# A three-part fused block on one core: operands of the channel stage recomputed or made in place instead of kept in DRAM

## The chip, the cores and the metric

The kernel runs on one core of one Trainium2 chip. The metric is device time in microseconds (us) of one execution, as the median of several runs. Three runs of the kernel before gave 974.24, 976.15 and 978.49 us. The profiled execution, from which every duration below is taken, took 970.43 us.

## The reference

The computation is three blocks, one after the other, on a batch of 4 with 448 tokens (S) and 768 channels, all in float32:

```python
# 1. attention, 12 heads of 64, scores capped with tanh
s = cap * tanh(scale * (q @ k.T) / cap);  x = softmax(s) @ v
# 2. gated block
h = relu(x @ w_in)                        # 768 -> 1024
x = (h * sigmoid(conv3(h, conv_w))) @ w_out   # -> 768
# 3. token and channel mixing
u = x + (relu(x.T @ w_tok1) @ w_tok2).T   # token stage, 448 -> 256 -> 448
y = u + relu(u @ w_ch1) @ w_ch2           # channel stage, 768 -> 1536 -> 768
```

The weights of blocks 2 and 3 come as float64 and have to be narrowed to float32 on the chip. The change is in the last line, the channel stage.

## The kernel before, in words

**Precision.** A float32 product is made of three fast matmuls: each operand is split into a rounded high part and the remainder (`split3`: high x high, high x low, low x high). A split costs one ScalarE copy (the high part) and one VectorE subtraction (the low part), and the split operand is twice as large as what it was made from.

**The channel stage.** The 1536 hidden channels are cut in three thirds t of four blocks; the batch in two pairs p of two elements. Six stages s run in the order (t, p) = (0,0), (0,1), (1,1), (1,0), (2,0), (2,1), so that between neighbours either the pair or the third changes. I call them s=0 to s=5. A stage has two halves:

- `up` runs twice, once for each unit u of two hidden blocks (u = 2t, 2t+1). A Strassen-like scheme makes the 2x2 block product with seven products of nine matmuls each (`product`, L888) instead of eight. It needs seven combinations of input blocks, the operands of the input ("B11", "T1" and so on, `UB`, made by `u_make`: L794 on ScalarE, L795 and L804 on VectorE, from loads of `u_d` into tiles `c`, L801), and seven combinations of weight blocks, the first weights' operands (`W1`, placed in tiles named wi_h and wi_l). VectorE adds the products up (L893) and ScalarE and VectorE make the split relu (`relu`, L879 and L880).
- `down` runs twice, for the two batch elements, over six blocks m of output channels: twelve matmuls (L926) from the split hidden values and the second weights (`w2`), then VectorE adds (L927) the partial result v, which was loaded from DRAM (L921), and stores it again (L928; `v_d`, in the last third `out`). v lies in one of four tiles that rotate (`temp`).

The tiles of one unit's seven W1 operands are used again by the unit of the next third; those of `w2` and of the input's operands likewise.

**What is kept in DRAM.** Three things are made once, stored split, and loaded when needed:

- `us_d`: the 21 operand tiles (seven by three k) of pair 0's input. They are stored as they are made (L797) and loaded for s=3, during the `down` of s=2 (`u_load`, L831), when the pair changes back from 1 to 0. For pair 1 they are made from `u_d` with `u_all`, each time.
- `w1_d`: the split W1 operands of units 2 to 5 (28 tiles). Units 0 and 1 go straight into place. The others are written to a staging tile (`staging`, two of them), stored (L639), and loaded in `down` of the last stage of a third (`w1_load`, L868).
- `w2_d`: the split second weights (24 halves), through staging (L673), loaded at the start of each third (`w2_load`, L874).

**Making weights.** A job narrows one 128x384 block (`block`: load L619, one ScalarE instruction L620, three VectorE instructions L621 to L623, into a tile ba, bb or bx, each one buffer deep), and then makes from it one or more splits (`parts`, L609 and L610) and sums. A unit takes four jobs, a block of second weights two. The jobs of the first third run during the token stage before. The 32 of the others are put into the program in the stages, at every step of `up` and `down`, in numbers that the table `JOBS` sets:

```python
JOBS = 5, 11, 9, 7, 0, 0
...
due += JOBS[s] / 26
while due >= 1:
    due -= 1
    wc_step(st_pools)
```

What is still left is flushed before the loads that need it.

**Order.** The program is written in the order of these loops, and the framework's scheduler lays out each engine's instructions from it, in one fixed order per engine. All DMAs of this part are issued by SP (SyncE) in one queue, in order: a DMA whose source is not ready holds up those behind it.

Of the kernel before, what the change touches and what calls it, by code (L numbers as in the profile page):

```python
# [20 lines left out]
KD = DM // 128  # L21
# [9 lines left out]
QK = S + KW  # L31
JOBS = 5, 11, 9, 7, 0, 0
YTB = 9
# [270 lines left out]
def fused_kernel(ctx, tc, ins, out, attention):  # L304
# [5 lines left out]
    v_d = [PRE.tile([B, KD, 128, S], F32, name=f"v_d{i}", tag=f"v_d{i}") for i in range(2)]  # L310
    w1_d = PRE.tile([MC // 2, 7, 128, 768], F32, name="w1_d")
    w2_d = PRE.tile([MC, 2, 128, 768], F32, name="w2_d")
    us_d = PRE.tile([7, 3, 128, 2 * S], F32, name="us_d")
    wide = {n: ins[n].bitcast(U32) for n in ("w_in", "conv_w", "w_out", "w_tok1", "w_tok2", "w_ch1", "w_ch2")}
# [311 lines left out]
    def unit_jobs(u):  # L626
# [4 lines left out]
        def put(name, t):  # L631
            o = ORDER.index(name)
            if u < 2:
                W1[u, o] = place_of(u, o)
                parts(t, W1[u, o])
            else:
                w = staging()
                parts(t, w)
                nc.sync.dma_start(w1_d[u, o], w.bitcast(F32))  # L639

# [27 lines left out]
    def w2_jobs(c):  # L668
        def job(pools, i):
            t = block(pools, wide["w_ch2"][c, :, 768 * i : 768 * i + 768], "bx")  # L670
            w = staging()
            parts(t, w)
            nc.sync.dma_start(w2_d[c, i], w.bitcast(F32))  # L673

        return [lambda pools, i=i: job(pools, i) for i in range(2)]

    def third_jobs(t):
        return [j for u in (2 * t, 2 * t + 1) for j in unit_jobs(u)] + [j for c in range(4 * t, 4 * t + 4) for j in w2_jobs(c)]

# [70 lines left out]
    while True:  # L750
# [6 lines left out]
        if n >= WCS and not begun:  # L757
            begun = True
            todo.extend(third_jobs(0))
        if n > TKS:  # L760
# [24 lines left out]

    def u_make(p, k, want, keep):


        def put(name, t):
            if name not in want:  # L790
                return
            o = BORDER.index(name)
            w = u_tile(o, k)
            nc.scalar.copy(w[:, 0], t)  # L794
            nc.vector.tensor_tensor(w[:, 1], t, w[:, 0].bitcast(F32), op=ALU.subtract)  # L795
            if keep:
                nc.sync.dma_start(us_d[o, k], flat(w).bitcast(F32))  # L797

# [24 lines left out]

    def u_all(p, want, keep):
        for k in range(3):
            yield from u_make(p, k, want, keep)

    def u_load():
        for o in range(7):
            for k in range(3):  # L830
                nc.sync.dma_start(flat(u_tile(o, k)).bitcast(F32), us_d[o, k])  # L831
                yield

    toks.append(tokens(B - 1))
    first = u_all(0, BORDER[0:3], True)
    while toks:
# [27 lines left out]

    def w1_load(u):
        for o in range(7):
            W1[u, o] = place_of(u, o)
            nc.sync.dma_start(W1[u, o].bitcast(F32), w1_d[u, o])  # L868

    def w2_load(c):  # L870
        pool = Gm if c % 4 < 2 else Gb
        w2[c] = pool.tile([128, 2, 2, 384], F32R, name=f"w2_{c % 4}", tag=f"w2_{c % 4}")
        for i in range(2):
            nc.sync.dma_start(w2[c][:, i].rearrange("p t n -> p (t n)").bitcast(F32), w2_d[c, i])  # L874

# [41 lines left out]
    def down(t, p, j):  # L917
        b = 2 * p + j
        for m in range(KD):
# [3 lines left out]
            for r in range(4):  # L923
                w, h = w2[4 * t + r][:, m // 3, :, m % 3 * 128 : m % 3 * 128 + 128], hs[r, j]
                for n, (l, x) in enumerate(split3(w[:, 0], w[:, 1], h[:, 0], h[:, 1])):
                    nc.tensor.matmul(ps[:, 0:S], l, x, start=r == 0 and n == 0, stop=r == 3 and n == 2)  # L926
# [3 lines left out]

    for _ in u_all(0, BORDER[3:7], True):
        pass
    for c in range(4):
        w2_load(c)
    todo.extend(third_jobs(1) + third_jobs(2))
    order = [(0, 0), (0, 1), (1, 1), (1, 0), (2, 0), (2, 1)]
    due = 0.0
    for s, (t, p) in enumerate(order):
        nt, np_ = order[s + 1] if s < 5 else (t, p)

        def tick():
            nonlocal due
            due += JOBS[s] / 26
            while due >= 1:
# [3 lines left out]
        for i in range(2):  # L948
            for n, _ in enumerate(up(2 * t + i)):
                if i == 0 and n == 0 and s and t != order[s - 1][0]:  # L950
                    wc_step(st_pools, len(todo) - 16 * (2 - t))
                    for c in range(4 * t, 4 * t + 4):
                        w2_load(c)
                tick()
        coming = iter(())
        if np_ != p:
            coming = u_load() if s == 2 else u_all(np_, BORDER, False)
        for j in range(2):
            for m, _ in enumerate(down(t, p, j)):
                for _ in range(2):  # L960
                    next(coming, None)
                if nt != t and m == 3:
                    wc_step(st_pools, len(todo) - 16 * (2 - nt) - 8)
                    w1_load(2 * nt + j)
                tick()
        for _ in coming:
            pass


# [73 lines left out]
```

## Time and profile before

| what | value |
|---|---|
| median of three runs | 976.15 us (974.24 to 978.49) |
| the profiled execution | 970.43 us |
| its span | 968.3 us |
| TensorE matmul busy (PE) | 887.6 us, 92% |
| VectorE busy (DVE) | 684.3 us, 71% |
| ScalarE busy (ACT) | 492.8 us, 51% |
| TensorE clock granted, mean | 0.966 of full speed |
| moved by DMA | 216.91 MB, mean 224 GB/s |

The span is the profiled execution from its first instruction to its last; 2.1 us lie around it. The chain that ended last is put to PE for 42% of the span, to DMA for 22%, to DVE for 20%, to ACT for 8%. In the slices of the span PE is at 9 tenths or more nearly everywhere, with two dips in the last 400 us (6 to 7 tenths), and the DMA engines are at 8 to 9 tenths through that part, where they stood at 1 to 7 before. Averages over the span say little here, because the last 400 us, the channel stage, are a stage of their own.

### The profile page before, as it was taken

To read this page: it belongs to the slowest core of one execution; us is meant where nothing else is said; L and a number is where in the kernel's file an instruction comes from. 1 tells how busy PE (TensorE), PEld (TensorE's weight loads), DVE (VectorE), ACT (ScalarE), POOL (GpSimd) and SP (SyncE) were. 2 spreads that over 40 slices of the span, in tenths; PEclk is the share of its full clock that TensorE was granted. 3 is DMA by queue.
4 is the path that set the end of the run, shared out by engine and by line. 5 is a ranking of instruction groups with operands and counts; after the bars stand their busy time and mean duration, and the time that the engine had idled before them with its cause. 6 is when DMAs were issued, how large, how long until landed. Compare 5 with 4: busy or idle time off the path is not lost.

```text
span 968.3 us, 12321 instructions
## 1 busy us (share of the span) xinstructions
PE 887.6 (92%) x4105; PEld 762.9 (79%) x4105; DVE 684.3 (71%) x1244; ACT 492.8 (51%) x817; POOL 4.2 (0%) x19
## 2 busy tenths in 40 slices
PE   7989999989999999989999797799996678999997
PEld 4655888868998898879888686689895567898996
DVE  6769989789866887468976655998648326749542
ACT  6979888777876787437543322444213102214210
POOL 0000000000000000000000000000000000000000
PEclk9999999989999999999999988899999889999999
DMA  7665555755155422573588889889999889897324
GB/s 270 202 212 186 174 187 176 246 197 168 57 181 208 156 91 66 176 231 114 170 282 298 301 295 353 269 275 338 302 321 301 312 297 328 295 338 233 120 86 146
DMA packets 95833, 216.91 MB, mean 224 GB/s; under 512 B 13618, under 2 KB 54546, under 8 KB 93458
## 3 DMA queue, kind: packets, MB, share of 16 engines
q1 hardware_dynamic: 95762, 216.05, 66.5%
q8 instruction: 34, 0.56, 0.2%
q14 instruction: 37, 0.30, 0.1%
HBM read 149.19 MB, written 63.90 MB: 220 GB/s over the span
## 4 chain that ended last, share of the span: by engine, by line
PE 42%; DMA 22%; DVE 20%; ACT 8%; issue 5%; SPq 3%; DVEq 0%; ACTq 0%
PE mm L926 9%; PE mm L488 7%; PE mm L462 6%; PE o L888 5%; DMA c<-u_d 3%; PE ps_s L146 2%; DMA w_raw<-in_w_out 2%; PE ps_s L147 2%; DMA u_d<-yt 2%; DMA rr<-v_d 2%; PE ps_e L722 2%; PE ps_e L736 1%; DMA raw<-in_qk 1%; DMA sel<-in_w_ch 1%; DMA w_raw<-in_w_ch 1%
## 5 line engine op out<-in xcount | busy, mean ns | idle before, releaser
L926 PE MATMUL mm<-hs,w 128*128 128x448 f32 x864 | 192.3, 380 | 29.3 <-DVE sums L927 14.2
L926 PEld LDWEIGHTS mm<-hs,w 128*128 128x128 f32 x864 | 167.0, 195 | 51.1 <-DVE sums L927 16.4
L488 PE MATMUL mm<-gh,wo 128*128 128x448 f32 x384 | 128.8, 376 | 7.2 <-ACT wo L358 3.5
L462 PE MATMUL mm<-xx,wi_h 128*128 128x448 f32 x384 | 115.2, 370 | 0.5 <-DVE xx L449 0.5
L488 PEld LDWEIGHTS mm<-gh,wo 128*128 128x128 f32 x384 | 73.2, 192 | 17.0 <-ACT wo L358 5.3
L146 PE MATMUL ps_s<-ab 128*128 128x448 f32 x192 | 82.5, 431 | 3.3 <-DVE ab L115 3.0
L462 PEld LDWEIGHTS mm<-xx,wi_h 128*128 128x128 f32 x384 | 71.8, 188 | 9.2 <-issue 2.0
L168 ACT ACTIVATE a<-ps_s,icap 128x896 f32<-128x896 f32 x76 | 66.9, 884 | 23.1 <-PE ps_s L147 18.6
L488 PE MATMUL mm<-gl,wo 128*128 128x448 f32 x192 | 71.7, 373 | 0.3 <-DVE gl L477 0.3
L147 PE MATMUL ps_s<-low,ab 128*128 128x448 f32 x192 | 71.4, 373 | 0.0
L169 ACT ACTIVATE a<-a,cap 128x896 f32<-128x896 f32 x76 | 70.2, 925 | 1.2
L462 PE MATMUL mm<-xx,wi_l 128*128 128x448 f32 x192 | 70.3, 366 | 0.0
L176 DVE TENSOR_TENSOR al<-a,ah 128x896 fp32r<-128x896 f32 (+1 forms) x56 | 54.4, 973 | 3.2
L888 PE MATMUL o<-u,wi_h 128*128 128x448 f32 x216 | 51.0, 368 | 1.5 <-ACT u L794 1.3
L175 DVE CAST ah<-a 128x896 fp32r<-128x896 f32 (+1 forms) x56 | 31.6, 566 | 28.8 <-ACT a L169 13.5
L888 PE MATMUL o<-u,wi_l 128*128 128x448 f32 x216 | 49.1, 364 | 2.5 <-DMA u<-us_d 0.9
L888 PE MATMUL o<-xx,wi_l 128*128 128x448 f32 x162 | 39.7, 375 | 8.5 <-ACT xx L794 5.3
L146 PEld LDWEIGHTS ps_s<-ab 128*128 128x128 f32 x192 | 36.7, 192 | 13.2 <-issue 5.5
L888 PEld LDWEIGHTS o<-u,wi_h 128*128 128x128 f32 x216 | 40.8, 190 | 6.2 <-ACT u L794 2.7
L888 PEld LDWEIGHTS o<-u,wi_l 128*128 128x128 f32 x216 | 40.2, 188 | 6.4 <-DMA u<-us_d 1.3
L111 ACT CAST ab<-raw 128x960 fp32r<-128x960 f32 x38 | 37.2, 989 | 15.8 <-DMA raw<-in_qk 9.7
L620 ACT ACTIVATE w_pt<-w_raw 128x384 f32<-128x384 f32 x32 | 17.6, 551 | 51.7 <-DMA w_raw<-in_w_ch 46.9
(161 smaller groups left out, 1677.2 us busy)
## 6 DMA issues: line engine op xcount, KB each, us to landing
raw<-in_qk SPq DMA_DIRECT2D x20, 960.0 KB
wo<-wo_d SPq DMA_DIRECT2D x18, 1024.0 KB
w_raw<-in_w_ch SPq DMA_DIRECT2D x32, 384.0 KB
c<-u_d SPq DMA_DIRECT2D x48, 224.0 KB
w_d<-wi_l SPq DMA_DIRECT2D x26, 384.0 KB
w_d<-wi_h SPq DMA_DIRECT2D x26, 384.0 KB
w<-w_d SPq DMA_DIRECT2D x24, 384.0 KB
w_raw<-in_w_in SPq DMA_DIRECT2D x16, 384.0 KB
```

The costliest lines, as they stand in the source:

```text
L111: nc.scalar.copy(h, r)
L146: nc.tensor.matmul(ps[:, bank, 0:S], a[:, keys], a[:, 0:S], start=start, stop=False)
L147: nc.tensor.matmul(ps[:, bank, 0:S], a[:, keys], low, start=False, stop=stop)
L168: nc.scalar.activation(a[:, 0:n], ps[:, 0:n, 0:S], AF.Tanh, scale=self.c["icap"])
L169: nc.scalar.activation(a[:, 0:n], a[:, 0:n], AF.Exp, scale=self.c["cap"])
L175: nc.vector.tensor_copy(ah[:, 0:n], a[:, 0:n])
L176: nc.vector.tensor_tensor(al[:, 0:n], a[:, 0:n], ah[:, 0:n].bitcast(F32), op=ALU.subtract)
L462: nc.tensor.matmul(ps[:, 0:S], w, v, start=k == 0 and n == 0, stop=k == KD - 1 and n == 2)
L488: nc.tensor.matmul(ps[:, 0:S], w, v, start=k == 0 and n == 0, stop=k == MF - 1 and n == 2)
L722: nc.tensor.matmul(ps[:, 0:384], l, r, start=c == 0 and n == 0, stop=c == NS - 1 and n == 1)
L888: nc.tensor.matmul(ps, l, r, start=k == 0 and n == 0, stop=k == 2 and n == 2)
L926: nc.tensor.matmul(ps[:, 0:S], l, x, start=r == 0 and n == 0, stop=r == 3 and n == 2)
```

## The change

- `u_load` and `us_d` go. At each change of the pair (s=0, s=2, s=4) the input's 21 operands are made anew with `u_all`, from twelve loads of `u_d`; it advances by one step per m of `down` where it advanced by two.
- `w1_d` and `w1_load` go. Each unit's jobs write their splits straight into the tiles of `W1`. The jobs of the next third's first unit enter the program when the first `up` of a third's last stage is through (its tiles are free then), those of the second unit after the second `up`.
- `w2_d` holds float32, not splits: a job stores its 128x384 block from the tile bx itself (half of the bytes). `w2_load` loads a whole block of 128x768 into a staging tile and splits it there, one ScalarE and one VectorE instruction of 128x768; for the later thirds it does that at steps 2 to 5 of the first `up`.
- `JOBS` goes. In s=0 and s=2 eight jobs of second weights are spread over 26 steps, in s=1 and s=3 the eight of the next third's units over 19.

```diff
-            if u < 2:
-                W1[u, o] = place_of(u, o)
-                parts(t, W1[u, o])
-            else:
-                w = staging()
-                parts(t, w)
-                nc.sync.dma_start(w1_d[u, o], w.bitcast(F32))
+            W1[u, o] = place_of(u, o)
+            parts(t, W1[u, o])
...
             t = block(pools, wide["w_ch2"][c, :, 768 * i : 768 * i + 768], "bx")
-            w = staging()
-            parts(t, w)
-            nc.sync.dma_start(w2_d[c, i], w.bitcast(F32))
+            nc.sync.dma_start(w2_d[c, :, 384 * i : 384 * i + 384], t)
...
-        return [j for u in (2 * t, 2 * t + 1) for j in unit_jobs(u)] + [j for c in range(4 * t, 4 * t + 4) for j in w2_jobs(c)]
+        return [j for c in range(4 * t, 4 * t + 4) for j in w2_jobs(c)]
...
-            if keep:
-                nc.sync.dma_start(us_d[o, k], flat(w).bitcast(F32))
...
-    def w1_load(u):
-        for o in range(7):
-            W1[u, o] = place_of(u, o)
-            nc.sync.dma_start(W1[u, o].bitcast(F32), w1_d[u, o])
...
         pool = Gm if c % 4 < 2 else Gb
-        w2[c] = pool.tile([128, 2, 2, 384], F32R, name=f"w2_{c % 4}", tag=f"w2_{c % 4}")
-        for i in range(2):
-            nc.sync.dma_start(w2[c][:, i].rearrange("p t n -> p (t n)").bitcast(F32), w2_d[c, i])
+        t = staging().bitcast(F32)
+        nc.sync.dma_start(t, w2_d[c])
+        w2[c] = w = pool.tile([128, 2, KD * 128], F32R, name=f"w2_{c % 4}", tag=f"w2_{c % 4}")
+        nc.scalar.copy(w[:, 0], t)
+        nc.vector.tensor_tensor(w[:, 1], t, w[:, 0].bitcast(F32), op=ALU.subtract)
...
+        due, rate = 0.0, 0.0
+        if s % 2 == 0 and t < 2:
+            todo.extend(third_jobs(t + 1))
+            rate = 8.5 / 26
...
             for n, _ in enumerate(up(2 * t + i)):
-                if i == 0 and n == 0 and s and t != order[s - 1][0]:
-                    wc_step(st_pools, len(todo) - 16 * (2 - t))
-                    for c in range(4 * t, 4 * t + 4):
-                        w2_load(c)
+                if s % 2 == 0 and s and i == 0 and 2 <= n < 6:
+                    w2_load(4 * t + n - 2)
                 tick()
-        coming = iter(())
-        if np_ != p:
-            coming = u_load() if s == 2 else u_all(np_, BORDER, False)
+            if nt != t:
+                todo.extend(unit_jobs(2 * nt + i))
+                rate = 8.5 / 19
+        coming = u_all(np_, BORDER) if np_ != p else iter(())
         for j in range(2):
             for m, _ in enumerate(down(t, p, j)):
-                for _ in range(2):
-                    next(coming, None)
-                if nt != t and m == 3:
-                    wc_step(st_pools, len(todo) - 16 * (2 - nt) - 8)
-                    w1_load(2 * nt + j)
+                next(coming, None)
                 tick()
...
+        wc_step(st_pools, len(todo))
```

Two places show how the orders differ. The first is SP's queue in the `down` of s=2. `v_d0` is what the stage before left of v, which is loaded to h0, h1, rr or sums and stored to `v_d1`. Before:

```order
L921 DMA rr_7073<-v_d0_82 128x448
L831 DMA u11_7090<-us_d_86 128x896
L639 DMA w1_d_84<-wi_l7_7125 128x768
L928 DMA v_d1_83<-rr_7073 128x448
L831 DMA u12_7092<-us_d_86 128x896
L921 DMA h0_7094<-v_d0_82 128x448
L831 DMA u20_7111<-us_d_86 128x896
L831 DMA u21_7113<-us_d_86 128x896
L928 DMA v_d1_83<-h0_7094 128x448
```

In the changed program, at the start of the same half (L900 loads v, L907 stores it, L789 loads the blocks of u):

```order
L900 DMA h1_6893<-v_d0_82 128x448
L789 DMA c_7020<-u_d_81 128x448
L789 DMA c_7022<-u_d_81 128x448
L900 DMA h0_6982<-v_d0_82 128x448
L900 DMA rr_6957<-v_d0_82 128x448
L789 DMA c_7024<-u_d_81 128x448
L900 DMA sums_6925<-v_d0_82 128x448
L907 DMA v_d1_83<-h1_6893 128x448
```

Before, the load for the next m stood behind the store of this one. Now four loads of v stand ahead of the first store, and between them are loads of u of 224 KB where loads of split operands of 448 KB and stores of W1 stood.

The second place is VectorE in the token stage, where jobs of second weights run beside the token work (yt, xx and hl are the token stage's). Before, after the last instruction on bx came the split into a staging tile, and then the next job was free to write bx:

```order
L622 SCALAR_TENSOR_TENSOR bx_4828<-w_raw_4826,bx_4828 128x384
L709 TENSOR_TENSOR xx_4803<-ps_d_4799,xx_4803 128x384
L623 SCALAR_TENSOR_TENSOR bx_4828<-w_pt_4827,bx_4828 128x384
L709 TENSOR_TENSOR xx_4810<-ps_d_4806,xx_4810 128x384
L610 TENSOR_TENSOR wi_h7_4834<-bx_4828,wi_h7_4834 128x384
L709 TENSOR_TENSOR xx_4823<-ps_d_4819,xx_4823 128x384
L621 TENSOR_SCALAR bx_4888<-w_pt_4887 128x384
```

In the changed program:

```order
L619 SCALAR_TENSOR_TENSOR bx_4823<-w_raw_4821,bx_4823 128x384
L699 TENSOR_TENSOR xx_4818<-ps_d_4814,xx_4818 128x384
L620 SCALAR_TENSOR_TENSOR bx_4823<-w_pt_4822,bx_4823 128x384
L701 TENSOR_TENSOR xx_4834<-ps_d_4830,xx_4834 64x384
L717 SCALAR_TENSOR_TENSOR hl_4664<-ps_e_4864,hh_4663 128x384
L618 TENSOR_SCALAR bx_4880<-w_pt_4879 128x384
```

The split is gone from here, and L618 may write bx again only when the store of bx to DRAM, issued after L620, has landed.

## Rows read from the trace of the kernel before

**Rows 1.** The page: span, and what the DMA engines moved over it.
```profile
span 968.3 us, 12321 instructions
...
DMA packets 95833, 216.91 MB, mean 224 GB/s; under 512 B 13618, under 2 KB 54546, under 8 KB 93458
```

**Rows 2.** Windows: busy us (and instructions) of each engine, granted clock, DMA share, GB/s.
```profile
460.00:574.00 114.00, 101.96 (x534) 92.68 (x535) 83.27 (x164) 46.88 (x99) 0.00 (x0) 0.96 0.80 268
574.00:657.50 83.50, 69.72 (x308) 60.32 (x307) 63.57 (x120) 30.35 (x59) 0.00 (x0) 0.92 0.88 302
657.50:711.90 54.40, 52.24 (x258) 47.86 (x257) 40.55 (x81) 16.49 (x33) 0.00 (x0) 1.00 0.93 314
711.90:804.60 92.70, 69.53 (x303) 59.90 (x303) 43.23 (x81) 17.49 (x33) 0.00 (x0) 0.89 0.90 309
804.60:858.20 53.60, 51.66 (x251) 46.32 (x250) 33.44 (x65) 13.15 (x25) 0.00 (x0) 1.00 0.93 319
858.20:908.40 50.20, 49.39 (x243) 45.24 (x243) 38.76 (x68) 16.36 (x30) 0.00 (x0) 1.00 0.75 251
908.40:962.40 54.00, 53.99 (x266) 49.41 (x264) 20.50 (x34) 5.70 (x10) 0.00 (x0) 1.00 0.32 103
```

**Rows 3.** Chain that ended last, 574 to 732 us: start, us, what.
```profile
711.89 16.02 PE o L888 x80
```

**Rows 4.** Timeline of PE: start, us, instruction, count, [idle before and its releaser].
```profile
626.18 11.56 PE L926 MATMUL mm<-hs,w 128*128 128x448 f32 x48 [2.16 <-DVE sums L927]
...
699.45 12.44 PE L926 MATMUL mm<-hs,w 128*128 128x448 f32 x60 [1.61 <-DVE sums L927]
...
752.26 4.48 PE L926 MATMUL mm<-hs,w 128*128 128x448 f32 x12 [9.39 <-DVE sums L927]
...
932.48 29.92 PE L926 MATMUL mm<-hs,w 128*128 128x448 f32 x144
```

**Rows 5.** Chain that ended last, 732 to 811 us (the down half of s=2).
```profile
746.05 5.44 DMA sums<-v_d
...
756.26 3.54 DMA rr<-v_d
759.90 0.64 DVE rr L927
760.55 0.32 SPq L928
...
761.40 3.96 DMA h<-v_d
```

**Rows 6.** Timeline of DVE at the start of s=0.
```profile
587.81 1.28 DVE L804 TENSOR_TENSOR c<-c 128x448 f32<-128x448 f32 x2 [4.67 <-DMA c<-u_d]
...
597.83 0.62 DVE L804 TENSOR_TENSOR c<-c 128x448 f32<-128x448 f32 x1 [4.60 <-DMA c<-u_d]
```

**Rows 7.** DMA issues, whole span: queue, count, KB each.
```profile
us_d<-u SPq DMA_DIRECT2D x12, 448.0 KB
...
wi_h<-w_d SPq DMA_DIRECT2D x14, 384.0 KB
```

**Rows 8.** Groups of DVE instructions by shape: count, busy us, mean ns, idle before.
```profile
L927 DVE TENSOR_TENSOR h<-mm,h 128x448 f32<-128x448 f32 x35 | 21.7, 621 | 20.6 <-PE mm L926 13.4 <-DMA h<-v_d 6.0 <-DMA h<-u_d 1.1
...
L623 DVE SCALAR_TENSOR_TENSOR bx<-w_pt,bx 128x384 uint32<-128x384 uint32 x24 | 13.3, 552 | 0.3
...
L610 DVE TENSOR_TENSOR wi_h<-bx,wi_h 128x384 fp32r<-128x384 f32 x16 | 8.9, 555 | 5.5 <-ACT wi_h L609 4.8 <-DMA h<-u_d 0.6
```

**Rows 9.** The same view over the whole span, the widest form.
```profile
L176 DVE TENSOR_TENSOR al<-a,ah 128x896 fp32r<-128x896 f32 x42 | 45.7, 1089 | 2.3
```

**Rows 10.** Waits of PE in the token stage, 460 to 574 us: us in total, times, longest.
```profile
PE ps_d L705 <- DMA yt<-y_d: 7.4, 3, 5.7
```

**Rows 11.** Chain that ended last, 495 to 575 us: stores to DRAM from issue to landing.
```profile
513.22 5.97 DMA u_d<-yt
...
531.74 3.00 DMA y_d<-c
```

More of the change, by code (lines that the diff above doesn't have):

```diff
@@ L31 @@
 QK = S + KW
-JOBS = 5, 11, 9, 7, 0, 0
 YTB = 9
@@ L310, in fused_kernel @@
     v_d = [PRE.tile([B, KD, 128, S], F32, name=f"v_d{i}", tag=f"v_d{i}") for i in range(2)]
-    w1_d = PRE.tile([MC // 2, 7, 128, 768], F32, name="w1_d")
-    w2_d = PRE.tile([MC, 2, 128, 768], F32, name="w2_d")
-    us_d = PRE.tile([7, 3, 128, 2 * S], F32, name="us_d")
+    w2_d = PRE.tile([MC, 128, 768], F32, name="w2_d")
     wide = {n: ins[n].bitcast(U32) for n in ("w_in", "conv_w", "w_out", "w_tok1", "w_tok2", "w_ch1", "w_ch2")}
@@ L758, in fused_kernel @@
             begun = True
-            todo.extend(third_jobs(0))
+            todo.extend(unit_jobs(0) + unit_jobs(1) + third_jobs(0))
         if n > TKS:
@@ L784, in u_tile, with u_make @@
         return t
-    def u_make(p, k, want, keep):
+    def u_make(p, k, want):
         def put(name, t):
@@ L822, in u_make, with u_all @@
         yield
-    def u_all(p, want, keep):
+    def u_all(p, want):
         for k in range(3):
-            yield from u_make(p, k, want, keep)
-    def u_load():
-        for o in range(7):
-            for k in range(3):
-                nc.sync.dma_start(flat(u_tile(o, k)).bitcast(F32), us_d[o, k])
-                yield
+            yield from u_make(p, k, want)
     toks.append(tokens(B - 1))
-    first = u_all(0, BORDER[0:3], True)
+    first = u_all(0, BORDER[0:3])
     while toks:
@@ L863, in temp @@
         return pools["sm"].tile([128, S], F32, name=name, tag=name)
-    def w1_load(u):
-        for o in range(7):
-            W1[u, o] = place_of(u, o)
-            nc.sync.dma_start(W1[u, o].bitcast(F32), w1_d[u, o])
     def w2_load(c):
         pool = Gm if c % 4 < 2 else Gb
-        w2[c] = pool.tile([128, 2, 2, 384], F32R, name=f"w2_{c % 4}", tag=f"w2_{c % 4}")
-        for i in range(2):
-            nc.sync.dma_start(w2[c][:, i].rearrange("p t n -> p (t n)").bitcast(F32), w2_d[c, i])
+        t = staging().bitcast(F32)
[3 more added lines that the diff above has]
+        nc.vector.tensor_tensor(w[:, 1], t, w[:, 0].bitcast(F32), op=ALU.subtract)
     def relu(r, j, src):
@@ L923, in down @@
             for r in range(4):
-                w, h = w2[4 * t + r][:, m // 3, :, m % 3 * 128 : m % 3 * 128 + 128], hs[r, j]
+                w, h = w2[4 * t + r][:, :, m * 128 : m * 128 + 128], hs[r, j]
                 for n, (l, x) in enumerate(split3(w[:, 0], w[:, 1], h[:, 0], h[:, 1])):
@@ L929, in down @@
             yield
-    for _ in u_all(0, BORDER[3:7], True):
+    for _ in u_all(0, BORDER[3:7]):
         pass
@@ L934, in fused_kernel @@
         w2_load(c)
-    todo.extend(third_jobs(1) + third_jobs(2))
     order = [(0, 0), (0, 1), (1, 1), (1, 0), (2, 0), (2, 1)]
-    due = 0.0
     for s, (t, p) in enumerate(order):
         nt, np_ = order[s + 1] if s < 5 else (t, p)
+        due, rate = 0.0, 0.0
+        if s % 2 == 0 and t < 2:
+            todo.extend(third_jobs(t + 1))
+            rate = 8.5 / 26
         def tick():
             nonlocal due
-            due += JOBS[s] / 26
+            due += rate
             while due >= 1:
```

## The prediction

> **What bounds the kernel now.** I read the page first, for the bytes: 216.91 MB in a span of 968.3 us [rows 1]. A mean over the span hides the stage that is changed, so I cut the trace where each stage s ends, that is where its 144 matmuls of `down` are complete; the pieces of these on PE's timeline, of which the last row is all of s=5 in one, give the cuts at 657.5, 711.9, 804.6, 858.2, 908.4 and 962.4 us [rows 4]. The windows between them are the main view [rows 2]. TensorE at full pace does 80 matmuls in 16.02 us, 0.200 us each [rows 3]. A stage has 126 matmuls of `up` and 144 of `down`, 270, so 54.0 us. What a window is longer than its count times 0.200 us is lost: 21.9, 2.8, 32.1, 3.4, 1.6 and 0.8 us for s=0 to s=5, together 62.6. (Counts at the cuts overlap by a few. From 574 to 962.4 are 388.4 us, less 1620 x 0.200 leaves 64.4, the same within 2.) The reader should see that s=1, s=3, s=4 and s=5 already run at TensorE's pace and that nearly all of the loss is in s=0 and s=2.
>
> Next, who keeps PE waiting there. In s=2 the chain goes load of v (5.44, 3.54, 3.96 us), VectorE's add (0.64), SP's store, next load of v [rows 5]: about 5 us for each m, where twelve matmuls need 2.4. VectorE is busy for 43.2 of 92.7 us, the DMA engines for 0.90 [rows 2]. So s=2 hangs on DMA, and the more since SP issues one load of v per store there. A wait costs twice: after 9.39 idle us the next twelve matmuls took 4.48 us where twelve at full pace take 2.4, and the granted clock of the window is 0.89 in the mean, so part of it ran at 1.2 instead of 2.4 GHz [rows 2, 4]. In s=0 it is mixed: DMA at 0.88, but VectorE busy for 63.6 of 83.5 us, more than PE's 54, and idle for 4.67 and 4.60 us before single loads of u [rows 2, 6].
>
> **The change, part by part.** *Bytes removed.* 21 operand tiles of 448 KB no longer go out and in, 19.3 MB; 28 W1 tiles of 384 KB likewise, 22.0 MB; the second weights' 24 halves of 384 KB shrink by half both ways, 9.4 MB; twelve loads of u of 224 KB are added, 2.8 MB; the sizes are those of the issues [rows 7]. Net 48 MB less of 217, nearly all in the last 400 us. In s=2, where 92.7 us at 309 GB/s moved 28.6 MB, 9.6 MB of operands, 5.5 MB of W1 stores and about 2.4 MB of weight loads go and 2.8 MB come: 14 MB, over 58 us 240 GB/s. The stage s=4 moved 251 GB/s, made its 21 operands anew and lost 1.6 us [rows 2]. It is the nearest row for what s=2 becomes.
>
> *VectorE's work.* Counted in the order of instructions, between the first add of a product and the last L927 of each stage, VectorE has 122, 81, 85, 61, 64 and 34 instructions before and 102, 91, 91, 75, 69 and 34 after. The operands of s=2 add 33 there; splits that moved or fell away make the rest. At 0.53 us each (63.57/120 in s=0 [rows 2]; single ones show 0.55 to 0.62 [rows 8]) that is 54, 48, 48, 40, 37 and 18 us. Two to four splits of 128x768 per third cost more: between 0.555 for 384 and 1.089 for 896 elements [rows 8, 9] I take 0.95, so 0.8 us more in a stage. No stage now asks more of VectorE than PE's 54 us, but s=0 asks as much. ScalarE's copies beside them lie under its load: it was busy for 30 of 83.5 us at most [rows 2]. If that cover failed, twelve copies of about 1 us would be 12 us at worst.
>
> *s=0.* Of VectorE's 19.9 idle us, the two waits for u are 9.3. I let them shrink to 3.2 each (a lightly loaded landing of 3.00 us [rows 11] and the issue), and keep the rest: 54.9 + 17 = 72 us, loss 10. Ends: 4 if the waits mostly go, 20 if none does. *s=2.* Four loads of v now stand ahead of the first store, so a load has some three blocks, 7 us, to land. Loss 5, as VectorE's 49 of 54 us leave little room; ends 2 (s=4's) and 16 (half of now). *s=1, s=3.* The weights' splits go straight into tiles that the `up` just done has freed; all of them stand early enough in VectorE's order, ahead of that stage's last adds. Losses 4 (2 to 6) and 3. *s=4, s=5.* Four more splits in s=4's `up`: 3 and 0.8. Sum 25.8 against 62.6: 36.8 us gained.
>
> *Token stage.* VectorE loses eight splits of 0.55 us, SP nine stores of operands, behind which loads of yt stood; PE's waits for yt were 7.4 us, one of 5.7 [rows 10]. What comes is a new wait: a job's block lies in bx, one buffer deep, and now the store to DRAM reads it. The next job's first VectorE instruction waits until that store has landed, and the token stage's xx and hl, on which PE waits, are queued behind it. The trace has no store of 192 KB; stores of 224 KB landed after 3.00 and 5.97 us [rows 11]. I take 3.00, since the traffic falls, and 0.32 for SP [rows 5]. Of the 24 stores the order leaves 0.6 to 14.6 us of VectorE's work between the last instruction on bx and the next; summing what is short of 3.3 gives 8.2 us in the token stage and 7 in the stages, the latter mostly beside adds that wait for PE anyway. VectorE is busy for 83 of 114 us in the token stage [rows 2], so I let this and the relief cancel: 0, with ends of -5 and +9.
>
> The Trainium skill speaks against this part: "DMA: Bandwidth & Descriptors", section "Anatomy of one DMA", has a fixed cost of about 2 us per DMA, mostly the confirmation of the last byte, longest with HBM as the target (it is given for the other issuing path). By its formula a 192 KB store takes 2.45 us, an estimate, and 24 of them fully exposed 59 us, more than the 36.8 gained; the trace's 3.00 and 5.97 us [rows 11] bear the cost out, and whether it is exposed is the third rival.
>
> **Sum.** 970.4 - 36.8 + 0 = 933.6 us for an execution like the profiled one. The median of the runs, 976.15, is 5.7 above it; with that, **939 us**.
>
> **The rivals.** *VectorE takes DMA's place.* If its in-order waits keep it at the 76% of s=0 (63.6/83.5) in every stage, s=1 and s=2 last 49/0.76 = 64.5 us and lose 10.5 each; losses 10, 10.5, 10.5, 3, 3 and 0.8 are 37.8, a gain of 24.8, and with the token stage's 8.2 us: 953.8, so 959. For it: s=0 before. Against it: s=1 before, which had 40.6 us of VectorE in its 54.4 and lost 2.8 [rows 2].
>
> *Nothing moves.* If loads of v are slow by latency and SP's order, not by load, s=0 loses 20 and s=2 28 still; 970.4 - 2.6 + 5.7 is 973. For it: 3.54 us is not far from 3.00. Against it: the order, where the loads now run ahead.
>
> *Slower, by the stores from bx.* If each lands as late as the 5.97 us, 6.3 with its issue, the shortfalls sum to 62 us (29 in the token stage, 8 in s=0, 25 from s=1 on), and if all of it reaches PE the time is 933.6 + 62 + 5.7 = 1001. It decides against the change from 36.8/24 = 1.5 us exposed per store. For it: seven of the eight stores in the token stage have only two to five VectorE instructions behind them. Against it: 5.97 was measured under traffic that the change cuts, and half of the stores have over 3 us of work behind them.
>
> **How the numbers follow.** Forecast 0.69, VectorE as the bound 0.16, nothing 0.06, slower 0.09. All of the good ends (losses 13, token stage -5) give 915.8, so 921. All of the bad ends of the forecast (losses 50, token stage +9) give 967, so 972; they hardly come together, and VectorE's rival at 959 lies within, so the range ends at 966. About 0.5%, 5 us, is what a measurement of this kernel can tell from no change: faster by more 0.85, within it 0.06, slower by more 0.09.
>
> **What the profile after would show.** If right: some 169 MB moved; s=2 in 55 to 62 us with DMA near 0.75 and PE at a granted clock of 1.00; s=0 near 72 us with VectorE above 75% busy; DVE waits on stores of bx of a few us in all. It would be wrong if PE in s=2 still waited for the add of v (L906 there) behind loads of v, if VectorE's waits for landed stores reached 1.5 us per store, or if PE waited at the start of s=2 or s=4 for weights (wi_h, wi_l) that are made too late.

## The result, and the profile after

The changed kernel takes 920.70 us (median of four runs, 915.61 to 920.92); the kernel before, timed beside it, 976.44 us (974.24 to 978.49). The ratio is 0.9417, with a 95% interval of 0.9378 to 0.9456. I had forecast 939 us with a range of 921 to 966: the direction is right, the gain is 18 us larger than the forecast, and the time lies just below the range. The profiled execution after took 920.92 us, so it stands at the median; the one before, 970.43 us, stood 5.7 below its own.

The page of the changed kernel, for the bytes, to be held against [rows 1]:

```profile
span 918.7 us, 12096 instructions
...
DMA packets 81719, 168.91 MB, mean 184 GB/s; under 512 B 12050, under 2 KB 57586, under 8 KB 79346
```

The 48 MB went as counted (169 MB was forecast). The windows between the ends of the stages, cut in the same way and with the same columns as [rows 2]; the first is the token stage, then s=0 to s=5:

```profile
460.00:570.70 110.70, 103.05 (x548) 94.03 (x548) 85.83 (x169) 48.97 (x101) 0.00 (x0) 0.98 0.78 250
570.70:631.50 60.80, 57.46 (x279) 51.35 (x278) 56.03 (x107) 24.74 (x47) 0.00 (x0) 1.00 0.76 243
631.50:690.90 59.40, 55.79 (x264) 51.38 (x264) 46.75 (x94) 20.45 (x40) 0.00 (x0) 0.94 0.65 195
690.90:748.30 57.40, 55.51 (x272) 50.47 (x271) 48.88 (x93) 22.20 (x41) 0.00 (x0) 1.00 0.71 223
748.30:803.00 54.70, 54.61 (x271) 50.56 (x271) 38.54 (x75) 16.14 (x31) 0.00 (x0) 1.00 0.47 149
803.00:857.70 54.70, 54.64 (x272) 50.59 (x271) 40.77 (x71) 18.40 (x33) 0.00 (x0) 1.00 0.48 149
857.70:912.70 55.00, 54.99 (x271) 50.34 (x269) 20.51 (x34) 5.70 (x10) 0.00 (x0) 1.00 0.31 101
```

Between the profiled executions the time came from three places: the channel stage starts 3.3 us earlier (570.7 for 574.0), s=0 is 22.7 us shorter and s=2 35.3 us. The other four are together 11.6 us longer (s=1 by 5.0, s=3 by 1.1, s=4 by 4.5, s=5 by 1.0): 49.7 us in all, and the executions differ by 49.5. A part of the give-back is only where the cuts fall. Before, the windows of s=1, s=3 and s=4 held 258, 251 and 243 matmuls [rows 2], since some of their products had been done in the stage before; after, 264, 271 and 272. So losses are a better measure than lengths: the window less 0.200 us [rows 3] for each matmul in it. After, they are 5.0, 6.6, 3.0, 0.5, 0.3 and 0.8 us, together 16.2, where before they were 62.6.

TensorE's waits in s=2 show what went. First the kernel before, 711.9 to 804.6 us (who waited for what: us in total, times, longest):

```profile
PE mm L926 <- DVE sums L927: 9.9, 2, 9.4
PE mm L926 <- DVE rr L927: 5.5, 2, 2.9
PE mm L926 <- DVE h L927: 4.4, 4, 2.0
PE o L888 <- DMA xx<-us_d: 2.4, 2, 1.8
PE o L888 <- DMA u<-us_d: 0.9, 1, 0.9
```

Then the changed kernel, 690.9 to 748.3 us:

```profile
PE mm L905 <- DVE sums L906: 1.2, 2, 0.7
PE mm L905 <- DVE h L906: 0.6, 1, 0.6
```

The 19.8 us that TensorE stood for the adds of v are 1.8, and the 3.3 us for loads of operands are gone. The rest of the loss of 32.1 us before, 9 us, was no wait: the 303 matmuls kept TensorE busy for 69.5 us where they need 60.6 at full pace, at a mean granted clock of 0.89 [rows 2]. The end of the chain of waits (start, us, what) is now TensorE alone, at 0.20 to 0.21 us for each matmul, for the last 77 us:

```profile
831.59 3.23 DMA sums<-v_d
834.91 0.64 DVE sums L906
835.59 22.15 PE mm L905 x108
857.74 25.20 PE o L867 x126
882.93 29.77 PE mm L905 x144
912.73 0.62 DVE h L906
```

### The profile page after: what moved, and what is told of

Read it like the earlier page. It is cut to its first block, busy times and chain, and to the rows that moved or that the text cites. A ratio compares the mean times of both kernels' runs of the same rounds, so it can differ in the third digit from the quotient of the medians.

```text
span 918.7 us, 12096 instructions
## 1 busy us (share of the span) xinstructions
PE 872.0 (95%) x4105; PEld 758.0 (83%) x4105; DVE 696.5 (76%) x1265; ACT 501.5 (55%) x826; POOL 4.4 (0%) x19
## 5 line engine op out<-in xcount | busy, mean ns | idle before, releaser
L905 PE MATMUL mm<-hs,w 128*128 128x448 f32 x864 | 182.6, 371 | 7.6 <-DVE h L906 5.3
L905 PEld LDWEIGHTS mm<-hs,w 128*128 128x128 f32 x864 | 163.6, 190 | 24.9 <-DVE h L906 6.4
L167 ACT ACTIVATE a<-ps_s,icap 128x896 f32<-128x896 f32 x76 | 66.8, 884 | 23.0 <-PE ps_s L146 18.5
L867 PE MATMUL o<-u,wi_h 128*128 128x448 f32 x216 | 48.6, 362 | 0.0
L110 ACT CAST ab<-raw 128x960 fp32r<-128x960 f32 x38 | 37.2, 989 | 19.2 <-DMA raw<-in_qk 13.2
L784 ACT CAST u<-c 128x448 fp32r<-128x448 f32 x48 | 27.1, 567 | 34.1 <-DVE c L792 18.7
L146 PEld LDWEIGHTS ps_s<-low,ab 128*128 128x128 f32 x192 | 36.8, 192 | 9.1 <-issue 5.4
```

Source lines behind the costliest of these rows:

```text
L110: nc.scalar.copy(h, r)
L146: nc.tensor.matmul(ps[:, bank, 0:S], a[:, keys], low, start=False, stop=stop)
L167: nc.scalar.activation(a[:, 0:n], ps[:, 0:n, 0:S], AF.Tanh, scale=self.c["icap"])
L867: nc.tensor.matmul(ps, l, r, start=k == 0 and n == 0, stop=k == 2 and n == 2)
```

## The experiments

Two questions were open after the result. Which of the three parts brings the gain, and where? And why did s=0 gain so much more than I allowed: through the 9.6 MB of stores of operands that left it, or because those stores no longer stand in SP's queue in front of loads?

**The three parts, alone and in pairs.** With the kernels before and after these are the eight combinations. Part 1 is the input's operands made anew, part 2 the first weights' operands made in place, part 3 the second weights as float32. Two smaller differences go with part 2 in these kernels: the new spread of the jobs, and the later place of `w2_load` in the later thirds. With parts 1 and 2 together, `u_all` also advances by one step per m where it advances by two with part 1 alone.

Part 1 alone, on the kernel before:

```diff
-    first = u_all(0, BORDER[0:3], True)
+    first = u_all(0, BORDER[0:3], False)
-    for _ in u_all(0, BORDER[3:7], True):
+    for _ in u_all(0, BORDER[3:7], False):
-            coming = u_load() if s == 2 else u_all(np_, BORDER, False)
+            coming = u_all(np_, BORDER, False)
```

> The kernel before with one part of the change alone: operands of pair 0 are neither stored nor loaded, but made anew in s=2. W1 and the second weights stay as before, with JOBS. The stores put back cost 13 us in the changed kernel, 4.4 of them before s=0. Theory now (in s=2 it is W1's 14 stores and the order of SP's queue around them that cost, the operands' loads only little): s=0 from 83.5 to 65 to 70 us, s=2 still above 80, 955 to 965 us. Rival (the operands' loads made s=2 long, as the prediction had it): s=2 under 70 us, 935 to 945 us.

Measured (f1_us_alone): 931.62 us, ratio 0.9534 (0.9473 to 0.9595).

Part 3 alone, on the kernel before:

```diff
-            w = staging()
-            parts(t, w)
-            nc.sync.dma_start(w2_d[c, i], w.bitcast(F32))
+            nc.sync.dma_start(w2_d[c, :, 384 * i : 384 * i + 384], t)
```

and `w2_load` as in the change.

> The kernel before with the float32 second weights alone (stores of half the bytes from bx, loads split on arrival). If its bytes matter: 962 to 970 us. If the new wait for bx's stores outweighs them: 976 us or more.

Measured (f2_w2_alone): 957.96 us, ratio 0.9828 (0.9752 to 0.9905).

Parts 1 and 3, both edits above together:

> The kernel before with both, operands made anew and float32 second weights; only W1 goes through DRAM and JOBS stays. Theory (W1 in place is what s=2 needs): s=2 above 75 us and 945 to 962 us. Rival (each part removes its bytes' share, 48 MB in all of which W1 has 22): about 976 - 55 x 26/48, so 946 with s=2 near 70.

Measured (f3_us_w2): 934.73 us, ratio 0.96 (0.9527 to 0.9673).

Part 2 alone: the changed kernel with `us_d`, its stores and `u_load` put back (the next diff) and the edit of part 3 reversed.

> The changed kernel with the operands through DRAM and the second weights split in DRAM as before; W1 in place alone remains, with the new spread of jobs. Theory (W1 in place made most of s=2's gain): s=2 65 to 72 us, 935 to 945 us. Rival (by bytes, 22 of 48 MB): about 950 us.

Measured (f4_w1_alone): 942.58 us, ratio 0.9652 (0.9593 to 0.9712).

Parts 2 and 3: the changed kernel, with the operands kept in DRAM as before.

```diff
+            if keep:
+                nc.sync.dma_start(us_d[o, k], flat(w).bitcast(F32))
-        coming = u_all(np_, BORDER) if np_ != p else iter(())
+        coming = (u_load() if s == 2 else u_all(np_, BORDER)) if np_ != p else iter(())
-                next(coming, None)
+                for _ in range(2 if s == 2 else 1):
+                    next(coming, None)
```

> The changed kernel with one part undone: pair 0's operands are stored split (21 stores of 448 KB) and loaded for s=3, as before; W1 in place and the float32 second weights stay. Theory (the operands' traffic and its place in SP's queue made most of the loss): s=0 goes from 60.8 to about 70 us and s=2 from 57.4 to about 75, so 945 to 955 us in all. Rival (W1's stores and loads made it, and VectorE's smaller work in s=0): at most 930 us, s=0 within 3 us of 60.8.

Measured (e1_no_us): 933.52 us, ratio 0.9574 (0.9519 to 0.963).

Parts 1 and 2: the changed kernel with the edit of part 3 reversed.

> The change without its third part: operands made anew, first weights made straight into place, second weights stored and loaded as two halves of 384 KB as before. It completes the eight combinations. If each part relieves the same resource and the first two suffice, the third is worth nothing here: 918 to 924 us, s=0 near 61 and s=2 near 58. If the third part still counts beside the other two (it was worth 17 alone and, beside operands made anew, minus 3): 926 to 935, with the loss in s=0 and s=2 again. If bx, which only the third part reads by a store, is a cost, this run is faster than the whole change: 912 to 917, token stage shorter.

Measured (g1_us_w1): 916.07 us, ratio 0.9417 (0.937 to 0.9465).

Each against the kernel before that was timed beside it: part 1 brings 43 us, part 2 32, part 3 17 (with an interval of 9 to 24); 1 and 2 together 58, 1 and 3 only 40, 2 and 3 42, all three 56. The parts do not add up. Of the ranges expected for these six runs, the lower one of f4_w1_alone and the lowest of g1_us_w1 held; f1_us_alone, f2_w2_alone and f3_us_w2 came out below all of theirs, e1_no_us between its two. My reading in f1_us_alone, that without part 2 s=2 would stay above 80 us, fell: it took 76.0. The stages say why the parts don't add up. Each row is worked out from a kernel's windows: the loss as above, and the MB as length times GB/s. The times are medians, but the losses are those of one profiled execution each. That execution lies within some 6 us of the median, except for part 1 alone, where it took 940.93 us, 9 more than the median; the losses of that row may be too large.

| parts | us | s=0: loss, MB, GB/s | s=2: loss, MB, GB/s |
|---|---|---|---|
| none | 976.44 | 21.9, 25.2, 302 | 32.1, 28.6, 309 |
| 3 | 957.96 | 21.2, 23.3, 285 | 24.4, 29.4, 308 |
| 2 | 942.58 | 19.8, 25.4, 307 | 8.9, 22.6, 314 |
| 2, 3 | 933.52 | 21.7, 23.5, 295 | 5.8, 19.2, 286 |
| 1 | 931.62 | 8.0, 18.5, 270 | 12.6, 24.1, 317 |
| 1, 3 | 934.73 | 7.8, 15.3, 227 | 10.4, 21.9, 299 |
| 1, 2 | 916.07 | 10.0, 18.2, 272 | 3.1, 15.9, 273 |
| 1, 2, 3 | 920.70 | 5.0, 14.8, 243 | 3.0, 12.8, 223 |

Two things are to be read from it. In s=0 only part 1 counts: with the operands stored the loss is 20 to 22 us whatever else is changed, without them 5 to 10. In s=2 part 1 and part 2 each take most of the same loss: 32.1 falls to 12.6 or 8.9 with either, and to 3.1 with both. That is why they don't add up. Part 3 alone gains 7.7 us of loss in s=2, and its channel stage starts 6.1 us earlier (567.9 for 574.0); it brings nothing that shows where part 1 is in.

How s=2 gained is less clear than which part did it. With part 1 or part 2 alone the DMA engines moved 317 and 314 GB/s there, no less than the 309 before. Before, the chain to the longest wait for v, 9.39 us [rows 4], went through SP's order: a store of W1, which could go out only when VectorE had made its split, stood right ahead of the load of v. The chain of the kernel before:

```profile
744.81 0.56 DVE wi_h L610
745.37 0.02 issue
745.38 0.32 SPq L639
745.71 0.34 issue
746.05 5.44 DMA sums<-v_d
```

With part 2 alone these stores are gone, but the loads of v still follow one store each and land no sooner. The chain of f4_w1_alone in s=2:

```profile
743.12 4.70 DMA h<-v_d
...
754.11 4.36 DMA rr<-v_d
...
765.91 5.06 DMA h<-v_d
```

TensorE waits there for adds of v for 4.2 us in all, and has products of the next stage to do in between. With part 1 alone several loads of v stand ahead, and these waits are 2.2 us at the 317 GB/s. So the bytes, the place of the loads in SP's queue and TensorE's other work may all have a share, and no run here takes away one of them alone in s=2. For s=0 there are such runs.

**Bytes or queue?** A store that waits for its operand holds up the loads behind it on SP; before, VectorE's waits for c in s=0 were of this place [rows 6]. First the changed kernel with the 21 stores put back, and nothing that reads them:

```diff
+            if keep:
+                nc.sync.dma_start(us_d[o, k], flat(w).bitcast(F32))
```

> The changed kernel with the 21 stores of pair 0's operands put back in their places, which nobody reads; the operands are still made anew for s=3. VectorE's work is the same as in the changed kernel. Theory (s=0 was long because SP's queue waited for operands at these stores, and the loads of u behind them came late): s=0 about 70 us, s=2 as in the changed kernel, 928 to 933 us. Rival (s=0 gained from VectorE's 20 instructions less): s=0 within 3 us of 60.8, 920 to 924 us.

Measured (e2_keep): 934.19 us, ratio 0.9564 (0.9507 to 0.9621). The stores alone cost 13 us, and s=0 has its old loss again, 22.0 us. As e1_no_us, which loads them for s=3 instead of making them anew, took 933.52, the loading costs no more than the making.

Then the same bytes without a wait, from an input:

```diff
-                nc.sync.dma_start(us_d[o, k], flat(w).bitcast(F32))
+                nc.sync.dma_start(us_d[o, k], ins["qk"][o // 6, o % 6, 0, :, 0 : 2 * S])
```

> As the run with the 21 stores put back, but each moves as many bytes from an input in DRAM, so that SP does not wait for an operand; the bytes it stores are others, and nobody reads them. If the bytes alone made s=0 long: s=0 about 70 us and 928 to 933 us, as with the real stores. If the wait in SP's queue did: s=0 within 3 us of 60.8, 920 to 924 us.

Measured (e3_dummy): 925.43 us, ratio 0.9478 (0.9424 to 0.9533). This run decides nothing, since with no operand to wait for, the scheduler moved all 21 transfers to between 30 and 141 us, far from s=0. Two better ones keep the place of the stores and take away one thing each. The first issues them from POOL, which issues nothing else there; the bytes stay, SP is free:

```diff
-                nc.sync.dma_start(us_d[o, k], flat(w).bitcast(F32))
+                nc.gpsimd.dma_start(us_d[o, k], flat(w).bitcast(F32))
```

> The whole change, with the 21 operand tiles of 448 KB stored to DRAM again (nothing reads them), but issued by POOL, which has nothing else to issue in this stretch, instead of SP. The bytes are those of e2_keep (934.2 us) at about the same time; a store that waits for its operand no longer holds up the loads of u, yt and v behind it on SP. Theory of the queue: 920 to 926 us, s=0 at 60 to 65, VectorE's waits for c near 1 us in s=0. Theory of the bytes: 931 to 938 us, s=0 near 78, VectorE's waits for c near 10 us.

Measured (g2_keep_pool): 935.73 us, ratio 0.9617 (0.957 to 0.9664). The second leaves the stores on SP behind their operands, and takes away 13 bytes of 14:

```diff
-                nc.sync.dma_start(us_d[o, k], flat(w).bitcast(F32))
+                nc.sync.dma_start(us_d[o, k, :, 0:64], flat(w).bitcast(F32)[:, 0:64])
```

> The whole change with 21 stores of operands from SP, each at its old place and with its old wait for the operand, but of 64 of the 896 columns: 32 KB in place of 448 KB, 0.7 MB in all in place of 9.6. The reverse of g2_keep_pool. Theory of the queue: still slow, 929 to 936 us, s=0 at 72 to 80. Theory of the bytes: 919 to 925 us, s=0 at 60 to 64.

Measured (g3_keep_thin): 922.08 us, ratio 0.9466 (0.9419 to 0.9513).

The queue can't carry the main part. By the medians, full stores off SP are as slow as full stores on SP, and thin stores on SP cost 1.4 us (5 by the ratios, whose intervals overlap). Windows of s=0 (columns as in [rows 2]), e2_keep:

```profile
575.10:655.10 80.00, 65.31 (x290) 55.62 (x289) 62.63 (x118) 29.52 (x55) 0.00 (x0) 0.94 0.88 292
```

g2_keep_pool:

```profile
576.30:648.90 72.60, 61.06 (x279) 52.90 (x278) 56.06 (x107) 24.91 (x47) 5.93 (x11) 0.95 0.85 287
```

g3_keep_thin:

```profile
568.00:633.40 65.40, 60.64 (x282) 51.38 (x281) 58.51 (x112) 26.64 (x49) 0.00 (x0) 1.00 0.79 247
```

The losses in s=0 are 22.0 us with full stores on SP, 16.8 with full stores on POOL, 9.0 with thin stores on SP and 5.0 without stores. Taking the bytes from the stores on SP gives back 13 us, taking the full stores off SP 5. So most of the 17 us are the bytes, and the place in SP's queue may have some 4 or 5 of them; these are single executions, and those of e2_keep and g3_keep_thin took 4 and 3 us more than their medians. The ranges that I had for s=0 in the last two runs (near 78 us, and 60 to 64) were both missed by a little, towards the queue.

The row of g2_keep_pool beside that of the changed kernel is the cleanest pair: 279 matmuls and 107 VectorE instructions in both, VectorE busy for 56.06 and 56.03 us, and 72.6 us against 60.8. What differs is eleven stores, 5.0 MB of the 6.0 by which the traffic differs (20.8 against 14.8). Neither VectorE nor ScalarE waited for one of these stores to land. VectorE's waits for loads of u between 570 and 635 us say where it lands. In g2_keep_pool:

```profile
DVE c L795 <- DMA c<-u_d: 8.1, 3, 4.3
```

and in the changed kernel:

```profile
DVE c L792 <- DMA c<-u_d: 0.6, 1, 0.6
```

The three loads of u on the chain of g2_keep_pool between 570 and 610 us took this long from issue to landing:

```profile
580.73 6.77 DMA c<-u_d
...
591.25 5.66 DMA c<-u_d
...
600.30 6.33 DMA c<-u_d
```

So the 17 idle us that I kept for VectorE in s=0 were mostly DMA load, reaching VectorE through loads that land late. It is not traffic as such that costs: s=1 and s=3 before ran at 0.93 of the DMA engines and lost 3 us each [rows 2]. As I read it, it costs where somebody waits for a load that was issued shortly before; no run tests that by itself.

**The store from bx.** The third rival's mechanism can be taken away by two tiles in turn in place of one:

```diff
-            t = block(pools, wide["w_ch2"][c, :, 768 * i : 768 * i + 768], "bx")
+            t = block(pools, wide["w_ch2"][c, :, 768 * i : 768 * i + 768], ("ba", "bb")[i])
```

> The changed kernel with the second weights' jobs alternating between two tiles (ba and bb, which the other jobs do not use then) instead of bx alone. Theory (the wait for a landed store costs PE time where it is long, 5.9 us once in s=1 and some in the token stage): VectorE's 12.0 us of waits for stores go to under 3, s=1 from 59.4 to about 55.5, 912 to 916 us. Rival (these waits lie beside others): 919 to 922 us.

Measured (e4_bx2): 915.65 us, ratio 0.9388 (0.933 to 0.9447). To size this, and part 3 with it, three kernels ran side by side on one chip, six times each. The change:

> The change itself, beside the next two on one chip, in more rounds. Theory that the store from bx costs: 4 to 6 us above h2_bx2 and h3_us_w1, so 0.941 of before against 0.936. Theory that it costs nothing that a measurement can tell: within 2 us of both.

Measured (h1_change): 920.48 us, ratio 0.9444 (0.9397 to 0.9491). The edit above:

> The change with two tiles in turn for the blocks of second weights, as in e4_bx2. Theory that the store from bx costs: 4 to 6 us below h1_change, near 915. Theory that it costs nothing: within 2 us of h1_change.

Measured (h2_bx2): 915.65 us, ratio 0.9393 (0.9352 to 0.9435). Parts 1 and 2 only:

> The change without its third part, as in g1_us_w1. If the third part's gain in bytes (9.4 MB) is worth something and only the store from bx spends it again, this is at h1_change's level and above h2_bx2. If the third part's bytes are worth nothing where the first two parts are there, this is at h2_bx2's level.

Measured (h3_us_w1): 917.79 us, ratio 0.9415 (0.9372 to 0.9458). The intervals against the kernel before overlap, since its own runs scatter by over 1%. With all ten runs of each kernel the means are 920.1 for the change, 915.5 with two tiles and 917.2 without part 3, with standard errors of 0.6 to 1.0. So the store from one tile costs 4 to 5 us. With it, part 3 looks like a loss of 2.9 us, a little over two standard errors; with two tiles it may bring 1 or 2, which these runs don't settle. The kernel with two tiles has the lowest mean found, clearly below that of the change.

The waits of VectorE for landed stores, 450 to 918 us, first in h1_change, then in h2_bx2:

```profile
DVE bx L618 <- DMA w_d<-bx: 15.2, 9, 5.6
```

```profile
DVE ba L618 <- DMA w_d<-ba: 1.4, 1, 1.4
```

**Stores on POOL.** If no load on SP stood behind a store that waits for VectorE, would more come back? With two tiles, and all stores of blocks, v and the output from POOL:

```diff
-            nc.sync.dma_start(w2_d[c, :, 384 * i : 384 * i + 384], t)
+            nc.gpsimd.dma_start(w2_d[c, :, 384 * i : 384 * i + 384], t)
...
-            nc.sync.dma_start((v_d[t] if t < 2 else out)[b, m], v)
+            nc.gpsimd.dma_start((v_d[t] if t < 2 else out)[b, m], v)
```

> The change with two tiles for the second weights' blocks (e4_bx2, 915.7 us) and, in addition, the stores of these blocks and of v and of the output issued by POOL instead of SP, so that no load on SP stands behind a store that waits for VectorE. Theory of the queue: what is left of the losses in s=0 to s=2 (10.5, 2.9 and 3.0 us in e4_bx2) shrinks, 903 to 912 us. Theory that VectorE's work bounds s=0 (56 us busy of 60.8): s=0 cannot go below about 58, 910 to 916 us. If POOL issues more slowly than SP and v is late: 918 to 930.

Measured (g4_bx2_pool): 931.43 us, ratio 0.9556 (0.9505 to 0.9607), 16 us worse than with two tiles alone and just above the highest of the ranges. As stores from POOL turn out to have a cost of their own (the last section), the run doesn't say what SP's order still costs. With the blocks' stores alone on POOL:

> h2_bx2 with only the 24 stores of blocks issued by POOL; v and the output stay on SP. It parts what g4_bx2_pool (931.4 us) did in one. If the stores of v and of the output on POOL made g4_bx2_pool slow: 912 to 917 here. If any large transfer issued by POOL does: 920 to 931.

Measured (h4_bx2_blocks_pool): 919.42 us, ratio 0.9422 (0.9381 to 0.9463). It lies between its two ranges: 3 to 4 us are the blocks' stores (by means and by medians), and some 12 those of v and the output; of the 12 about 8 lie after the last store (the last section).

## Why the prediction was right or wrong

**Bytes, and s=2: right in size.** 169 MB; s=2 in 57.4 us (55 to 62 forecast, 59 as its value) with DMA at 0.71 (near 0.75) and the granted clock at 1.00. Its loss was put at 5 and is 3.0. I had given two reasons, four loads of v ahead of the first store and less traffic. TensorE's waits for adds of v went as both of them say, from 19.8 us to 1.8, but the runs don't part them. That these waits were 2.2 us with part 1 alone, at 317 GB/s, speaks for the order of the loads. So the number was right, and which of the reasons made it is open. TensorE did not wait for weights that are made too late: in s=2 it waited for adds alone, in s=4 for 0.1 us in all.

**VectorE's count: right.** Windows of 107, 94, 93, 75, 71 and 34 instructions against a count of 102, 91, 91, 75, 69 and 34; busy for 56, 47, 49, 39, 41 and 21 us against 54, 48, 48, 40, 37 and 18. The last two stages were 3 to 4 us too low, and it cost nothing there.

**s=0: the step that failed.** It said: "I let them shrink to 3.2 each ..., and keep the rest: 54.9 + 17 = 72 us, loss 10." The two waits for u went from 9.3 us to 0.6, and the rest, which I kept without a reason, did not stay either: VectorE was idle for 4.8 of 60.8 us and busy for 92%. The loss is 5.0 where I had 10, near the end of 4 that I had given for it; the other 6 us of the stage's length are matmuls on the other side of the cut. The landing of 3.00 us that I called lightly loaded was none: from 531 to 535 us the DMA engines were at 0.77. A better sum takes the idle time as the traffic's. The stage moved 25.2 MB at 302 GB/s in 83.5 us [rows 2]. The 14.8 MB that were left need 49 us at that rate, less than VectorE's 56 and TensorE's 55.8 us of work, and then that work is the bound, not VectorE's old idle time. In the four rows of the table without the stores, the larger of the MB at 302 GB/s and VectorE's busy time (56 to 63 us) falls 5 to 7 us short of the stage; VectorE's time with 17 us added is 9 to 13 too long.

**s=3 and s=4: too dear.** I put 3 us on each and they lost 0.5 and 0.3: 5.2 us too much together. They had lost 3.4 and 1.6 at 319 and 251 GB/s [rows 2], and their traffic fell to 149 GB/s; that this is why they lose less was not tested.

**s=1: too cheap.** 4 forecast, 6.6 lost. In this execution nearly all of it is one place, where the cost of the store from bx shows. VectorE's timeline there:

```profile
672.37 0.56 DVE L620 SCALAR_TENSOR_TENSOR bx<-w_pt,bx 128x384 uint32<-128x384 uint32 x1
...
682.26 0.36 DVE L618 TENSOR_SCALAR bx<-w_pt 128x384 uint32<-128x384 uint32 x1 [5.94 <-DMA w_d<-bx]
682.54 0.62 DVE L906 TENSOR_TENSOR h<-mm,h 128x448 f32<-128x448 f32 x1
```

SP's queue at the same time:

```profile
670.92 0.46 SPq L907 DMA_DIRECT2D v_d<-sums  x1
675.09 0.32 SPq L900 DMA_DIRECT2D h<-u_d  x1
...
676.88 0.48 SPq L663 DMA_DIRECT2D w_d<-bx  x1
```

And TensorE:

```profile
683.21 7.72 PE L905 MATMUL mm<-hs,w 128*128 128x448 f32 x24 [3.61 <-DVE h L906]
```

bx was ready at 672.93 us, but its store stood behind a load that SP could issue only at 675.09, went out at 676.88 and had landed at 682.26. VectorE, and with it the add that TensorE needed, stood for 5.94 us. TensorE waited for 3.61, and then took 0.32 us for each of 24 matmuls where it takes 0.20, 2.9 us more: the granted clock of the window of s=1 is 0.94, the only one of s=0 to s=5 after the change that is not at 1.00. With two tiles this wait is gone and s=1 loses 3.9 (e4_bx2) and 2.5 us (h2_bx2).

**The token stage: nearly right.** I had 0 (8.2 us for the stores from bx against as much relief); it is 3.3 us faster. With two tiles the channel stage starts 1.9 to 7.0 us earlier still (568.8 in h2_bx2, 563.7 in e4_bx2), so the stores seem to have had a cost there. But these two are executions of one kernel and 5.1 us apart, so the 3.3 us lie within the scatter, and how large either term was is not shown.

**The rivals.** *VectorE takes DMA's place* is half true: in s=0 VectorE has as much work as TensorE (56.0 and 55.8 of 60.8 us), but it is busy for 92%, not 76%, and in the other stages it has more room (at most 49 of 57 us). *Nothing moves* fell in its number (with the losses that it and the forecast give, its sum is 972, not 973); its mechanism, SP's order, was on the chain of s=2 before, and is there no more. *Slower, by the stores from bx* has its mechanism and not its size. VectorE waited 12.0 us in all for landed stores in the profiled execution (15.2 in h1_change), 0.5 us for each of the 24 where 1.5 decides; 4 to 5 us of them reached the time. The Trainium skill's fixed cost ("DMA: Bandwidth & Descriptors", section "Anatomy of one DMA"), by which I had estimated 2.45 us for such a store, is if anything low here: the one above landed after 5.4 us, and those that POOL issued in g4_bx2_pool after 4.2. What hides the rest is, by the count in the prediction, the work between two blocks; only one of these waits was followed to TensorE.

**The sum.** By the losses I had 25.8 us left and 16.2 are: s=0 5.0, s=2 2.0, s=3 and s=4 5.2 too much, s=1 2.6 too little. With 3.3 from the token stage that makes 12.9 us. The rest of the 18.3 between 939 and 920.7 is, within rounding, the 5.7 us that I added because the profiled execution before stood below its median; the one after does not. Runs of the kernel before scatter from 968 to 982 us, and what sets that was not tried. So s=0 is the step whose reasoning failed, with 5.0 us of the miss; s=3 and s=4 together (5.2) and the 5.7 for the scatter were as large.

## What to carry to other kernels

Where a stage hangs on DMA, don't keep the idle time of the other engines in a forecast with less traffic: here s=0 fell to within 5 us of VectorE's work, not to that work plus its old idle time. Savings that relieve the same stage can be one gain, not several; price each alone and together. A buffer that becomes the source of a store to DRAM may need a second one beside it (4 to 5 us here), and to tell bytes from queue order, move a transfer to another queue and, in another kernel, cut its size.

## What was not expected of the hardware

Stores from POOL ended late here. The last DMA issue on SP of the changed kernel (span 918.7 us), then the last one on POOL of g4_bx2_pool (span 932.1 us):

```profile
913.38 0.33 SPq L907 DMA_DIRECT2D out_t<-h  x1
```

```profile
918.41 0.54 POOL L907 DMA_DIRECT2D out_t<-h  x1 [1.94 <-DVE h L906]
```

From the last issue to the end of the span are 5.3 us on SP and 13.7 on POOL, while POOL's stores of this size and tile land after 2.7 us in the median (below); what fills the rest of the 13.7 us the trace doesn't show. An issue takes 0.54 us on POOL against 0.33 on SP. The Trainium skill ("Trainium Kernel Development and Optimization", section "Key Constraints") says that issuing from several engines only saves the sequencer's issue time; here, with the loads left on SP, it cost, and the time went from 915.65 to 931.43 us. The DMA issues of g4_bx2_pool (count, KB, median us to landing) also show that a landing is not one number: the same 224 KB take 3.6 us in the median in s=0 to s=3, where the changed kernel moves 243 to 149 GB/s, and 2.7 in s=4 and s=5, where it moves 149 and 101:

```profile
v_d<-h POOLq DMA_DIRECT2D x24, 224.0 KB, 3.6
...
out_t<-h POOLq DMA_DIRECT2D x12, 224.0 KB, 2.7
w_d<-ba POOLq DMA_DIRECT2D x12, 192.0 KB, 4.2
```
